# Re-laying the buffers behind the middle stage: eight output buffers for the last inverse products instead of four

## The chip, the cores and the metric

The kernel runs on one core of a Trainium2 chip. A core has a matrix engine (TensorE, PE in the profile; its weight loads stand apart as PEld), two elementwise engines (VectorE, DVE; ScalarE, ACT), GpSimd (POOL), and SyncE (SP), which here only issues DMAs. ACT and POOL issue DMAs too; ACTq and POOLq are their issues. Each engine works through its own instructions in the order of the program and stops at the first one whose inputs or buffers are not ready. Sixteen DMA engines move data between DRAM and the on-chip memory; matmul results land in PSUM banks, which an engine has to copy out.

The metric is the time of one execution in microseconds, lower being better; several runs are given as their median.

## What is computed

Two layers, A and B, each applied twice to `x` of 2048 rows and 576 columns, in the order A, B, A, B:

```python
x = x + _A_ref(_layernorm(x, axis=-1), ...)   # A: Cr @ (x Wr^T) - Ci @ (x Wi^T), a two-dimensional DFT's real part
x = x + _B_ref(_layernorm(x, axis=-1), B_k, B_v, B_shift_k, B_ssm_k, B_ssm_D)
# B: kv = (short convolution of k) * v
#    y  = (long causal convolution of kv with ssm_k, by FFT) + kv * ssm_D
#    return q * y                     # q is the layer-normed x
```

`y` depends on `k`, `v` and the convolution kernels alone, not on `x`. So it is worked out once, and used by both B layers.

## The kernel before

The long convolution (`branch()`) is woven into the first A layer (`layer()`). The A layer runs over 128 steps n: four blocks of 512 output rows, two parts (real and imaginary) and 16 row tiles. A step multiplies a row tile of `x`, kept in `mats` as a high and a low half, by one 128x512 piece of the DFT matrix: twelve matmuls of 512 columns into the PSUM tiles `s0` to `s3`, and two into `rm`. The DFT pieces are loaded by SP (`load_c`), one a step, and split into halves by ACT (line 98) and DVE (line 99). After each block come eight half pieces of `hidden()`, 27 matmuls of 288 columns each, with an addition by DVE on line 287.

The convolution goes through three stages: a first transform (up to step 42), the middle stage, and the last inverse. Middle and last stage are one list, `feeds`: 64 middle items (two column halves `hf`, 32 groups `qg`) and 32 last-inverse products (two halves, 16 columns `j`). Ten of the products stand between the later middle items. The other 22 follow the last middle item: six of half 0 and all sixteen of half 1. `branch()` is a generator, and the loop over the steps draws from it as the share of the A layer that has passed demands, so that it ends near step 111.

A middle item (`mid_kernel`, `mid_signal`, `mid_round`, `mid_inverse`, lines 520 to 549) uses two buffers `kk`, two `yf`, the constants `mc`, and an output buffer `vo` that it stores to `vd`.

A last-inverse product (`i2_products`, line 551) does, for each of its two 288-column pieces: two matmuls into a bank `bk`; a copy of that bank by ACT into a buffer `vo` (line 512 is the helper `act`, which keeps ACT's copies in their written order); a DMA from ACT's queue that writes one half of the buffer's partitions to `yb` in DRAM (line 561); and a DMA from POOL's queue that adds the other half onto the same rows of `yb` (line 564). The addition has to wait for the write, and the buffer is free again only when the addition has landed. A product therefore takes two `vo` buffers, of which there are four, one ring shared with the middle stage.

Its inputs: SP loads a column from `vd` into a `land` buffer (`load_feed`), ACT and DVE split it into `df` (lines 512 and 518), and POOL loads its coefficients into an `fc` buffer (`load_fc`, line 172).

After the products, `make_x1` gates the rows of `x` with `yb` (load on line 168, `gated` with lines 669 and 672), from step 113 on. The first two rows use buffers in `flts`, on the words that held `land`, `kk` and part of `vo`; later rows use the region `gate`, on the words of the middle stage's region `mid`. The tile `rt`, into which line 272 copies, and the third buffer of the DFT pieces (`craw`) lie on words of the four old `vo` buffers.

The program's order on each engine is not that of the source: a scheduler places the instructions by its own estimate of when each can run, and the hardware then keeps that order. `issue_after` and `behind` add orderings to it. Waits on DMAs go by a small set of semaphores that the DMAs of a kind take in turn.

The lines that the change touches stand in `branch()`, in the loop over `feeds`, under `if i == last_mid`:

Of the kernel before, what the change touches and what calls it, by code (L numbers as in the profile page):

```python
# [10 lines left out]
F32 = mybir.dt.float32  # L11
# [4 lines left out]
P = 128  # L16
HP = P // 2
S = 2048
D = 576
# [3 lines left out]
HD = D // 2  # L23
# [42 lines left out]
def fnet_h3_kernel(ctx: ExitStack, tc: tile.TileContext, x, c_mat, w_re, w_im, k_pad, v, shift_k,  # L66
# [45 lines left out]
    def flat(words, dt, name):  # L112
        return sb.tile([P, words], dt, tag=name, name=name)
# [4 lines left out]
    def region_b(dt, name):  # L118
        return sb.tile([P, 6 * WIDE], dt, tag="rb", name=name)
# [9 lines left out]
    ring = {}  # L129

    def lay(t, at, *sizes):

        for name, words, n in sizes:
            ring.setdefault(name, Ring()).tiles.extend(t[:, at + i * words:at + (i + 1) * words] for i in range(n))
            at += n * words
        assert at <= t.shape[1], (at, t.shape, sizes)
        return at

    def fresh(*names):
        for name in names:  # L140
            ring[name] = Ring()
# [14 lines left out]
    flts = flat(FLT, F32, "flts")  # L156
# [192 lines left out]
    def branch():  # L349
# [3 lines left out]
        at = lay(flts, SC_AT + CRAW * NT, ("so", D, 4), ("land", D, 3))  # L353
# [129 lines left out]
        m1 = region_b(FR, "mid")  # L483
        kk_at = SC_AT + CRAW * NT + 4 * D
        at = lay(m1, 0, ("df", 2 * D, 3), ("mc", 4 * P, 1))
        fresh("land", "fc")
        old = ring["craw"]
        held = [t for t in (old() for _ in range(3)) if t is not old.tiles[CRAW]]
        fresh("craw")
        ring["craw"].tiles.extend(held)  # L490
        spare = at
        at = lay(m1, at, ("yf", D, 2))
        fc_at = at
        at = lay(flts, SC_AT + CRAW * NT, ("res", D, 2))
# [25 lines left out]
        def mid_kernel(df):  # L520
            pk, kk = mid_half(df, HD), two(ring["kk"]())
            act(kk[:, 0, :], pk[:, :HD], AF.Copy)
            act(kk[lo, 1, :], kk[hi, 0, :], AF.Copy, scale=-1.0)
            act(kk[hi, 1, :], kk[hi, 0, :], AF.Copy)
            act(kk[hi, 0, :], kk[lo, 0, :], AF.Copy)
            return kk

        def mid_signal(df, kk):
            px = mid_half(df, 0)
            p1, p2 = kk[:, 0, :], kk[:, 1, :]  # L530
            nc.vector.tensor_tensor(p1, px[:, :HD], p1, OP.mult)
            nc.vector.tensor_tensor(p2[lo], px[hi, :HD], p2[lo], OP.mult)
            nc.vector.tensor_tensor(p2[hi], px[lo, :HD], p2[hi], OP.mult)
            nc.vector.tensor_tensor(p1, p1, p2, OP.add)
            return p1

        def mid_round(p1):
            yf = two(ring["yf"]())
            act_split(yf[:, 0, :], yf[:, 1, :], p1)
            return yf  # L540

        def mid_inverse(hf, qg, yf):
            pv = bank()
            mm(pv[:, :HD], mc[:, 2, :], yf[:, 0, :], True, False)
            mm(pv[:, :HD], mc[:, 2, :], yf[:, 1, :], False, False)
            mm(pv[:, :HD], mc[:, 3, :], yf[:, 0, :], False, True)
            vo = ring["vo"]()
            act(vo, pv[:, :HD], AF.Copy)
            nc.scalar.dma_start(v_d[hf][4 * qg:4 * qg + 4].rearrange("m j d -> (m j) d"), vo)

        def i2_products(hf, j, fc, vf):
            cols = slice(hf * HD, (hf + 1) * HD)
            late = []
            for i in range(2):
                ps, yo = bank(), ring["vo"]()
                cs = slice(i * HD, (i + 1) * HD)
                mm(ps[:, :HD], fc[:, i, :], vf[0][:, cs], True, False)
                mm(ps[:, :HD], fc[:, i, :], vf[1][:, cs], False, True)
                act(yo, ps[:, :HD], AF.Copy)
                to = yb_d[j][i::2, cols]  # L560
                nc.scalar.dma_start(to, yo[i * HP:(i + 1) * HP])
                late.append((to, yo[(1 - i) * HP:(2 - i) * HP]))
            for to, corr in late:
                nc.gpsimd.dma_start(to, corr, accum_op=OP.add)  # L564
# [13 lines left out]
        def load_feed(i):  # L578
            if i < len(feeds):
                kind, hf, q = feeds[i]  # L580
                landed[i] = ring["land"]()
                load_after(two(landed[i]) if kind else landed[i], v_d[hf][:, q::J, :] if kind else
                           t_d[4 * q:4 * q + 4, :, hf * D:(hf + 1) * D].rearrange("m j d -> (m j) d"))

        def load_fc(k):
            if k < len(rows):
                fcs[k] = two(ring["fc"]())
                load_fr(fcs[k], i2c[rows[k]])

        def split_feed(i):  # L590
            if i < len(feeds):
                halves[i] = parts("df")
                act_split(*halves[i], landed.pop(i))
# [10 lines left out]
        for i, (kind, hf, q) in enumerate(feeds):  # L604
            df = halves.pop(i)
            if kind:
                i2_products(hf, q, fcs.pop(used), df)
                load_fc(used + ahead)
                used += 1
            else:  # L610
                if len(yfs) == MID_LAG:
                    mid_inverse(*yfs.pop(0))
                    yield 0.4
                kk = mid_kernel(df)
                if product is not None:
                    yfs.append((*product[:2], mid_round(product[2])))
                yield 1.6
                product = hf, q, mid_signal(df, kk)
            split_feed(i + 2)
            if i >= I2_FIRST - 8 and feed_ahead == 3:  # L620
                tiles = [ring["land"]() for _ in range(3)]
                if tiles[0] is third:
                    ring["land"], feed_ahead = Ring(tiles[1:]), 2
                    lay(m1, fc_at, ("fc", 2 * P, 2))
                    load_fc(0)
                    load_fc(1)
            if feed_ahead == 2:
                feed_ahead = 2.5
            else:
                load_feed(i + int(feed_ahead) + 2)  # L630
            if i == last_mid:
                yield 0.4
                mid_inverse(*yfs.pop(0))
                yfs.append((*product[:2], mid_round(product[2])))
                while yfs:
                    yield 0.4
                    mid_inverse(*yfs.pop(0))
                for name, t, at, words in (("fc", m1, spare, 2 * P), ("land", flts, kk_at, D)):
                    old = ring[name]
                    held = [old.tiles[(old.n + m) % 2] for m in range(2)]  # L640
                    fresh(name)
                    lay(t, at, (name, words, 2))
                    ring[name].tiles.extend(held)
                for m in range(2):
                    load_fc(used + ahead + m)
                    load_feed(i + ahead + 3 + m)
                ahead = feed_ahead = 4
            yield I2_COST if kind else 1.1
# [101 lines left out]
    pending = []  # L750
    lay(flts, SC_AT, ("craw", NT, CRAW))
    br = branch()
    wl = load_w()
    load_x(0)
# [21 lines left out]
    for n, whole in layer(get_x0, lambda j: x[:, j, :], done0, pending):  # L776
# [3 lines left out]
        if (whole or whole is not None and n % J < J - 1) and n <= F1_END and not part:  # L780
            at = n if whole else n - 0.5
# [26 lines left out]
        if m == 0:  # L808
            lay(flts, SC_AT + CRAW * NT + 2 * D, ("xa", D, 2), ("yb", D, 2))
            old = ring["craw"]  # L810
            held = [old(), old()]
# [203 lines left out]
    for n, whole in layer(get_x1, lambda j: xb_d[j], done1, pending, 1):  # L1015
# [4 lines left out]
        if n == 0:  # L1020
            for name, at in (("xa", 0), ("yb", 4 * D)):
                old = ring[name]
# [5 lines left out]
        if n == STATIC:  # L1028
            t7.append(region_a(FR, "t7"))
            at = lay(flts, SC_AT + CRAW * NT, ("csum", WIDE, 3), ("rems", 2 * REM, 2))  # L1030
            lay(flts, SC_AT, ("csum", WIDE, 1))
            old = ring.pop("cs")
# [126 lines left out]
```

## Time and profile before

| What | Value |
|---|---|
| Median of 3 runs | 1223.32 us (1223.09 to 1223.67) |
| The profiled execution's own time | 1227.15 us |
| Its span | 1225.4 us |
| PE busy | 1179.6 us, 96% |
| DVE, ACT, POOL busy | 839.0, 671.8, 130.6 us |
| Mean DMA rate over the span | 212 GB/s |
| Granted TensorE clock, mean | 0.989 |

Times in the trace are microseconds from the span's start. "Idle before, releaser" says how long an engine stood still before an instruction and what ended the wait. In the chain of work that ended last, each step is followed back to what released it. Matmul ends are modelled, and a matmul's row (about 390 ns for 512 columns) is longer than the distance between two of them in a dense stream, so that short gaps can lie inside "busy". The granted clock is the share of full speed that TensorE was given.

### The profile page before, as it was taken

To read this page: it belongs to the slowest core of one execution; us is meant where nothing else is said; L and a number is where in the kernel's file an instruction comes from. 1 tells how busy PE (TensorE), PEld (TensorE's weight loads), DVE (VectorE), ACT (ScalarE), POOL (GpSimd) and SP (SyncE) were. 2 spreads that over 40 slices of the span, in tenths; PEclk is the share of its full clock that TensorE was granted. 3 is DMA by queue.
4 is the path that set the end of the run, shared out by engine and by line. 5 is a ranking of instruction groups with operands and counts; after the bars stand their busy time and mean duration, and the time that the engine had idled before them with its cause. 6 is when DMAs were issued, how large, how long until landed. Compare 5 with 4: busy or idle time off the path is not lost.

```text
span 1225.4 us, 18167 instructions
## 1 busy us (share of the span) xinstructions
PE 1179.6 (96%) x6184; PEld 992.8 (81%) x6184; DVE 839.0 (68%) x1498; ACT 671.8 (55%) x1343; POOL 130.6 (11%) x180
## 2 busy tenths in 40 slices
PE   7999999999999999997889999999999999999995
PEld 5776667988898888885668898888888888889995
DVE  7899973788877677762236756675776777775663
ACT  7855655688867778763344667544444445541200
POOL 2210000000000112104541111000000000001110
PEclk9999999999999999999889999999999999999998
DMA  9779898455666667558877777772682687895511
GB/s 338 279 218 312 265 291 257 148 161 176 216 205 204 188 182 211 176 182 214 192 169 227 244 242 245 251 265 91 178 290 90 198 279 259 260 319 173 195 68 39
DMA packets 152574, 260.37 MB, mean 212 GB/s; under 512 B 17185, under 2 KB 61473, under 8 KB 152482
## 3 DMA queue, kind: packets, MB, share of 16 engines
q1 hardware_dynamic: 106770, 205.45, 52.3%
q10 hardware_dynamic: 33680, 42.63, 10.2%
q0 software_dynamic: 12032, 11.15, 5.4%
q8 instruction: 48, 0.79, 0.2%
q14 instruction: 44, 0.36, 0.1%
HBM read 187.80 MB, written 71.37 MB: 211 GB/s over the span
## 4 chain that ended last, share of the span: by engine, by line
PE 47%; DMA 8%; DVE 3%; ACT 2%; issue 2%; POOL 0%; ACTq 0%; POOLq 0%; DVEq 0%; SPq 0%
PE s L75 28%; PE bk L75 18%; DMA yb<-flts 6%; PE rm L75 2%; ACT flts L512 1%; DVE mats L99 1%; DMA t<-ud 1%; ACT mats L98 0%; DMA flts<-td 0%; DMA flts<-vd 0%; DVE flts L181 0%; ACT u L98 0%; DMA y<-flts 0%; ACT mid L512 0%; DVE gate L669 0%
## 5 line engine op out<-in xcount | busy, mean ns | idle before, releaser
L75 PE MATMUL s<-mats 128*128 128x512 f32 x2088 | 546.8, 396 | 2.2 <-ACT mats L195 0.8
L75 PEld LDWEIGHTS s<-mats 128*128 128x128 f32 x2088 | 382.3, 189 | 85.0 <-issue 10.9
L99 DVE TENSOR_TENSOR mats<-flts,mats 128x512 fp32r<-128x512 f32 x206 | 140.8, 688 | 72.3 <-ACT mats L98 62.0
L98 ACT ACTIVATE mats<-flts 128x512 fp32r<-128x512 f32 x206 | 128.3, 628 | 79.8 <-PE bk L75 31.0
L75 PE MATMUL bk<-mid 128*128 128x288 f32 x704 | 132.5, 305 | 20.1 <-ACT flts L512 13.5
L75 PEld LDWEIGHTS bk<-mid 128*128 128x128 f32 x704 | 109.7, 189 | 47.3 <-ACT flts L512 23.5
L518 DVE TENSOR_TENSOR mid<-flts,mid 128x576 fp32r<-128x576 f32 (+1 forms) x149 | 93.6, 628 | 58.1 <-ACT mid L512 55.1
L512 ACT ACTIVATE flts<-bk 128x288 f32<-128x288 f32 x192 | 74.4, 405 | 104.5 <-DMA yb<-flts 47.3
L75 PE MATMUL bk<-w,u 128*128 128x288 f32 x864 | 124.2, 300 | 2.0 <-ACT w L240 1.0
L75 PEld LDWEIGHTS bk<-w,u 128*128 128x128 f32 x864 | 120.6, 192 | 6.6 <-ACT flts L512 2.9
L75 PE MATMUL rm<-mats 128*128 128x512 f32 x304 | 96.0, 393 | 0.0
L512 ACT ACTIVATE flts<-flts 64x288 f32<-64x288 f32 x192 | 85.0, 443 | 5.7 <-ACT flts L512 0.3
L512 ACT ACTIVATE mid<-flts 128x576 fp32r<-128x576 f32 (+1 forms) x148 | 80.1, 574 | 5.6 <-DMA flts<-td 2.1
L184 POOL TENSOR_TENSOR flts<-flts 128x1 f32<-128x1 f32 x35 | 29.3, 836 | 502.4 <-DVE flts L183 500.5
L451 ACT ACTIVATE flts<-bf 128x384 f32<-128x384 f32 (+1 forms) x104 | 43.2, 463 | 45.6 <-PE bf L75 45.5
L75 PE MATMUL bk<-mats 128*128 128x288 f32 (+1 forms) x376 | 67.8, 317 | 0.0
L75 PEld LDWEIGHTS rm<-mats 128*128 128x128 f32 x304 | 57.4, 189 | 11.9 <-issue 0.2
L75 PE MATMUL s<-t,mats 128*128 128x512 f32 x264 | 65.2, 390 | 0.1
L564 POOL DMA_DIRECT2D yb<-flts x64 | 54.0, 899 | 88.2 <-DMA yb<-flts 37.8
L75 PE MATMUL bk<-mats,t 128*128 128x288 f32 (+1 forms) x368 | 59.3, 303 | 0.0
L75 PEld LDWEIGHTS bk<-mats 128*128 128x128 f32 x376 | 55.6, 188 | 3.4
L75 PEld LDWEIGHTS s<-t,mats 128*128 128x128 f32 x264 | 49.4, 188 | 10.9 <-DVE t L99 0.7
(146 smaller groups left out, 1492.0 us busy)
## 6 DMA issues: line engine op xcount, KB each, us to landing
flts<-in_c_mat SPq DMA_DIRECT2D x148, 256.0 KB, 3.6
ph<-in_c_mat SPq DMA_DIRECT2D x54, 512.0 KB, 4.4
flts<-in_c_mat SPq DMA_DIRECT2D x30, 512.0 KB, 5.1
flts<-td SPq DMA_DIRECT2D x53, 288.0 KB, 3.0
td<-flts ACTq DMA_DIRECT2D x36, 384.0 KB, 4.6
vd<-flts ACTq DMA_DIRECT2D x64, 144.0 KB, 2.3
flts<-vd SPq DMA_DIRECT2D x32, 288.0 KB, 3.8
ud<-ph ACTq DMA_DIRECT2D x12, 512.0 KB, 6.4
```

The costliest lines, as they stand in the source:

```text
L75: return nc.tensor.matmul(ps, lhsT, rhs, start=first, stop=last, skip_group_check=more).ins
L98: a = nc.scalar.activation(h, src, AF.Copy).ins
L99: return a, nc.vector.tensor_tensor(l, src, h.bitcast(F32), OP.subtract).ins
L184: pows.append(nc.gpsimd.tensor_tensor(rs, ve, mhalf, OP.pow).ins)
L451: stored[:] = [nc.scalar.activation(so[:, i, :], ps[i], AF.Copy).ins]
L512: last_act.append(nc.scalar.activation(*args, **kw).ins)
L518: nc.vector.tensor_tensor(l, src, h.bitcast(F32), OP.subtract)
L564: nc.gpsimd.dma_start(to, corr, accum_op=OP.add)
```

## The change

When the last middle item is through, three kinds of its words are free: `yf` (1152 words a partition), `mc` (512) and `kk` (1152). Before, `yf` became two more `fc` buffers and `kk` two more `land` buffers. After the change, `mc` becomes the two `fc` buffers, `yf` the two `land` buffers, and `kk` four more `vo` buffers. The 22 products that follow have eight `vo` buffers, of which the new four are taken first. The number of `fc` and `land` buffers (four each) stays the same; no computing instruction and no DMA is added or removed.

```diff
                 while yfs:
                     yield 0.4
                     mid_inverse(*yfs.pop(0))
-                for name, t, at, words in (("fc", m1, spare, 2 * P), ("land", flts, kk_at, D)):
+                for name, t, at, words in (("fc", m1, spare - 4 * P, 2 * P), ("land", m1, spare, D)):
                     old = ring[name]
                     held = [old.tiles[(old.n + m) % 2] for m in range(2)]
                     fresh(name)
-                    lay(t, at, (name, words, 2))
+                    lay(t.bitcast(F32) if name == "land" else t, at, (name, words, 2))
                     ring[name].tiles.extend(held)
+                old = ring["vo"]
+                held = [old() for _ in range(4)]
+                fresh("vo")
+                lay(flts, kk_at, ("vo", HD, 4))
+                ring["vo"].tiles.extend(held)
                 for m in range(2):
                     load_fc(used + ahead + m)
                     load_feed(i + ahead + 3 + m)
```

## The prediction

> **What bounds the kernel now.** I read the page's busy times and its chain of waits first.
>
> ```profile
> PE 1179.6 (96%) x6184; PEld 992.8 (81%) x6184; DVE 839.0 (68%) x1498; ACT 671.8 (55%) x1343; POOL 130.6 (11%) x180
> PE s L75 28%; PE bk L75 18%; DMA yb<-flts 6%; PE rm L75 2%; ACT flts L512 1%; DVE mats L99 1%; DMA t<-ud 1%; ACT mats L98 0%; DMA flts<-td 0%; DMA flts<-vd 0%; DVE flts L181 0%; ACT u L98 0%; DMA y<-flts 0%; ACT mid L512 0%; DVE gate L669 0%
> ```
>
> TensorE is the bound over all, but the writes and additions into `yb` hold 6% of the chain, about 74 us of 1225.4, and they can only lie where the last inverse runs. So the next view is busy time by stretches: late middle stage, the 22 products from about 546 us, and what follows. The first number is the length, the others are each engine's busy time, and the last three are the granted clock, the DMA share and GB/s.
>
> ```profile
> 391.00:546.00 155.00, 153.26 (x840) 131.96 (x839) 112.45 (x216) 115.26 (x254) 23.02 (x31) 1.00 0.67 190
> 546.00:580.00 34.00, 26.54 (x143) 21.39 (x143) 8.46 (x13) 12.75 (x27) 14.75 (x21) 1.00 0.89 217
> 580.00:620.00 40.00, 32.05 (x149) 25.11 (x148) 10.42 (x16) 15.11 (x33) 21.03 (x28) 0.89 0.90 205
> 620.00:643.00 23.00, 19.87 (x96) 16.82 (x95) 7.67 (x12) 9.53 (x20) 9.87 (x13) 0.82 0.71 141
> 643.00:688.00 45.00, 44.84 (x198) 36.59 (x196) 28.14 (x73) 23.30 (x45) 7.92 (x13) 1.00 0.70 221
> ...
> 546.00:643.00 97.00, 78.47 (x385) 63.32 (x385) 26.56 (x39) 37.40 (x79) 45.65 (x61) 0.91 0.85 194
> ...
> 612.00:620.00 8.00, 4.91 (x18) 3.20 (x17) 1.28 (x2) 2.81 (x7) 3.07 (x4) 0.89 1.02 271
> ```
>
> PE is dense before 546 and after 643. Between them it is idle for 97.0 - 78.5 = 18.5 us even with modelled ends, no engine is full, and the clock drops. Who waits there:
>
> ```profile
> ACT flts L512 <- DMA yb<-flts: 47.3, 29, 3.1
> ...
> PE bk L75 <- ACT flts L512: 12.1, 13, 1.9
> ...
> PE bk L75 <- ACT mid L512: 6.3, 7, 1.9
> ```
>
> ACT stands for 47.3 us in front of a copy into `vo` until an addition has landed, PE for 18.4 us behind ACT. The chain in order of time (start, length) shows one turn of a buffer, then the last write; the timeline gives the first and last copy, the first matmul of step 112, and ACT's wait after the products:
>
> ```profile
> 550.02 2.57 DMA yb<-flts
> ...
> 557.31 4.42 DMA yb<-flts
> ...
> 562.28 3.42 DMA yb<-flts
> 565.73 0.04 issue
> 565.77 0.42 ACT flts L512
> 566.22 2.88 DMA yb<-flts
> ...
> 640.82 1.94 DMA yb<-flts
> ```
>
> ```profile
> 549.58 0.71 ACT L512 ACTIVATE flts<-bk 128x288 f32<-128x288 f32 x2 [2.88 <-DMA flts<-vd]
> ...
> 640.38 0.41 ACT L512 ACTIVATE flts<-bk 128x288 f32<-128x288 f32 x1
> ...
> 642.88 6.30 PE L75 MATMUL s<-mats 128*128 128x512 f32 x27
> ...
> 649.18 0.60 ACT L272 ACTIVATE flts<-rm 64x512 f32<-64x512 f32 x1 [8.39 <-DMA yb<-flts]
> ```
>
> A write is issued at 557.31, its addition at 562.28, the buffer is copied into again at 565.77 and the next write goes out at 566.22: a turn of 8.9 us. From the first copy to the last it is 640.38 - 549.58 = 90.8 us for 21 steps from product to product, 4.32 us each, or two products in 8.6 us. Four buffers, two a product, one turn: the ring is the bound.
>
> **The change, part by part.** Nothing is computed or moved more or less, so the price is in waits alone.
>
> *The added `vo` buffers.* With eight, a copy waits for the addition of four products back instead of two, and the built program's waits say so. A turn of 8.6 us would give 8.6 / 4 = 2.15 us a product. But the built order of ACT does not allow that. It puts the writes of a product behind the copies of the next one, sometimes the next two: the copies of product 5 and of product 7 stand before the last write of 5, and 7 needs the addition of 3. Followed through, a chain of such waits leads from product 3 to 15 in four turns, so three products a turn: 8.6 / 3 = 2.87 us. Three in flight also load the DMA engines and POOL's queue more than two, so I lengthen the turn by about 1.3 us to 9.9, which is an estimate inside what the chain of before shows (a single one of its DMA pieces runs from 2.57 to 4.42 us above). That gives 3.3 us a product.
>
> *What each engine would need.* Work by shapes in 546 to 643 (count | busy us, mean ns), and two dense runs of matmuls from a later stretch of the chain:
>
> ```profile
> L564 POOL DMA_DIRECT2D yb<-flts x43 | 36.6, 900 | 38.7 <-DMA yb<-flts 14.7 <-ACT flts L512 10.8 <-ACT mats L98 10.6
> L75 PE MATMUL s<-mats 128*128 128x512 f32 x117 | 35.4, 418 | 0.0
> L75 PE MATMUL bk<-w,u 128*128 128x288 f32 x158 | 25.1, 321 | 0.7 <-ACT flts L512 0.7
> ...
> L75 PE MATMUL bk<-mid 128*128 128x288 f32 x90 | 23.5, 343 | 17.9 <-ACT flts L512 11.5 <-ACT mid L512 6.3
> ...
> L512 ACT ACTIVATE flts<-bk 128x288 f32<-128x288 f32 x45 | 18.2, 410 | 52.6 <-DMA yb<-flts 47.3 <-DMA flts<-vd 2.9 <-PE bk L75 2.1
> ...
> L172 POOL DMA_DIRECT2D mid<-in_i2c x18 | 12.6, 714 | 14.5 <-PE bk L75 12.6 <-DMA yb<-flts 1.7 <-PE rm L75 0.2
> L75 PE MATMUL rm<-mats 128*128 128x512 f32 x20 | 7.7, 429 | 0.0
> ```
>
> ```profile
> 701.76 2.73 PE s L75 x12
> ...
> 704.95 3.60 PE bk L75 x27
> ```
>
> Dense, a matmul of 512 columns takes 2.73 / 12 = 0.228 us and one of 288 takes 3.60 / 27 = 0.133. So PE needs (117 + 20) x 0.228 + (158 + 90) x 0.133 = 31.2 + 33.0 = 64 us of the 97. POOL issues 36.6 + 12.6 = 49.2 us, or 2.2 a product. ACT is busy for 37.4 us; its 44 write issues take its turn as well, but stand partly beside its copies. None of these reaches 3.3 us a product.
>
> *From the pace to the time.* Call the pace p. In the built order the last product comes a step earlier than before: behind it PE still has two plus two matmuls of 512, a run of 27 and a full step of 14 before step 112 begins: 4 x 0.228 + 3.60 + 14 x 0.228 = 7.7 us, less about 0.5 for the copy that follows the product's matmuls. Step 112 then begins at 549.6 + 21p + 7.2, where it began at 642.9. The gain is 642.9 - 556.8 - 21p = 86.1 - 21p. With p = 3.3 it is 16.8 us. From 643 on PE is dense (44.8 of 45.0), so the gain is carried to the end.
>
> *`land` in place of `yf`, `fc` in place of `mc`.* The new `land` loads now wait, in SP's queue, for PE's last `mid_inverse`, as the new `fc` loads did before; behind them in SP's queue stand DFT pieces. Before, those loads waited for the last rounding, just ahead of that matmul. I take nothing: the half-1 loads next in the queue had to wait in any case for the last store to `vd`, which comes after the same matmul. Bounds: 0 to 2 us, one matmul wait of PE (1.9) at most. `mc` is free with the same matmul as `yf`: nothing.
>
> *The gating's first rows, `rt` and `craw`.* The first two rows load `yb` into the words of `kk`, which now hold the buffers of products 14 and 15, so these loads wait in SP's queue for the last additions, and DFT pieces from step 117 on stand behind. The addition that ACT waited for at 649.18 landed 8.8 us after the last copy at 640.38; 8.8 us after the new last copy is 1.6 us into step 112. Step 117 comes 5 x 14 x 0.228 = 16 us after 112 begins. So this wait is covered; if the cover were gone, each microsecond past it would cost one. `rt` and the third `craw` buffer lie on the old buffers, which are no longer the last ones used: ACT's wait of 8.4 us on line 272 shrinks to a microsecond or two. PE did not stand for it before, so I count nothing.
>
> Sum: -16.8 us in the profiled execution (1227.15, span 1225.4). The median stands 3.8 us below that execution: 1223.3 - 16.8 = 1206.5, say 1206.5.
>
> **Rivals.** *The other limits are lower than I think.* If later products find their buffers free and PE is all but dense, the 64 us of PE's work replace 97, a gain of 33 us at the very best. For it: none of the engines is full. Against it: three products a turn. With the turn unchanged, p = 2.87, the gain is 25.8 and the time 1197.5.
>
> *The DMA engines become the bound.* They are at 0.85 over the stage, 82 us of packets in 97. If packets keep their lengths and the share cannot pass 1.0, then with about 5 us of that traffic outside the products p is 77 / 22 = 3.5, or 3.73 if all of it counts; the gain is 12.6 or 7.8, the time 1210.7 or 1215.5. Against it: 8 us from 612 on moved 271 GB/s at 1.02, 1.4 times the stage's 194, so the lengths hold much waiting. [...]
>
> *Slower: packets lengthen under the crowding.* The same place; the price is 21 us for each microsecond of pace, and the break-even is p = 86.1 / 21 = 4.1, because the order leaves a whole step of PE's work behind the last product. It takes packets 4.1 / 3.73 = 1.10 times as long as now. With today's pace of 4.32 the time would be 1223.3 + 4.6 = 1227.9. Against it: 271 GB/s in the window above.
>
> *The change doesn't do what it says.* The waits of the built program have moved from two products back to four; only ACT's order could undo that, as priced.
>
> **How the numbers follow.** Pace from the turn, 3.1 to 3.5 us (1202 to 1211): 0.45. Close to the engines' limits, below 3.1 (1190 to 1202): 0.2. DMA-bound, 3.5 to 3.95 (1211 to 1220): 0.24. Above 3.95: 0.11, of which 0.04 within 0.2% (2.4 us, about what a measurement of this kernel can tell from no change) and 0.07 slower. So 0.89 faster, 0.04 the same, 0.07 slower. The range 1196 to 1218 leaves out about 0.06 below and 0.14 above.
>
> **What would show it.** ACT's wait for `yb` in the stage falls from 47 us to 15 or less; first to last copy takes about 69 us instead of 90.8; the DMA share of the stage rises above 0.95 and GB/s to about 240; the granted clock stays near 1.0; the wait on line 272 falls below 3 us; PE stays dense after step 112. I am wrong if ACT's wait for `yb` stays above 25 us (ACT's order or longer packets took the gain), if PE stands after step 112 for a DFT piece (SP held by the gating loads), or if POOL's additions queue behind `fc` loads that wait for PE.

## The result, and the profile after

| | Before | After |
|---|---|---|
| Median, same chip | 1223.49 us (1223.09 to 1225.22, 4 runs) | 1206.01 us (1205.11 to 1206.39, 4 runs) |
| Ratio, 95% interval | | 0.9853 (0.9836 to 0.987) |
| Profiled execution, its span | 1227.15, 1225.4 us | 1206.39, 1204.6 us |
| First to last copy of the 22 products | 90.8 us, 4.32 a product | 67.1 us, 3.19 a product |
| Step 112 begins | 642.88 us | 622.63 us |
| From there to the end of the span | 582.5 us | 582.0 us |

The change takes 17.5 us off the median, about 1.5%; 1206.5 was forecast. Two more pairs, each on a chip of its own, gave 1206.2 against 1225.49 (ratio 0.9843, 95% interval 0.9817 to 0.9869) and 1208.55 against 1226.41 (0.9851, 0.9829 to 0.9873).

The page of the kernel after: busy times, and the shares of the chain that ended last, by line.

```profile
PE 1169.3 (97%) x6184; PEld 989.5 (82%) x6184; DVE 838.6 (70%) x1498; ACT 669.8 (56%) x1343; POOL 129.7 (11%) x180
...
PE s L75 41%; PE bk L75 28%; PE rm L75 4%; DMA yb<-flts 3%; ACT flts L512 1%; ACT mid L512 1%; DMA t<-ud 1%; POOL yb L564 0%; DMA xa<-flts 0%; ACT u L98 0%; ACT mats L98 0%; ACTq L561 0%; DVE t L99 0%; POOLq L1160 0%; ACT t L98 0%
```

The writes and additions into `yb` hold 3% of the chain, where it was 6%. The same stretches as before: the stage now ends at 623 instead of 643.

```profile
391.00:546.00 155.00, 153.59 (x845) 132.62 (x844) 112.08 (x216) 115.40 (x254) 22.95 (x31) 1.00 0.67 191
546.00:580.00 34.00, 30.57 (x177) 26.17 (x177) 11.18 (x17) 16.57 (x37) 19.16 (x27) 1.00 1.03 263
580.00:623.00 43.00, 37.03 (x203) 32.19 (x202) 14.09 (x21) 18.44 (x42) 27.75 (x36) 0.96 0.99 225
546.00:623.00 77.00, 67.60 (x378) 58.36 (x378) 25.26 (x38) 35.02 (x78) 46.91 (x63) 0.98 1.01 242
623.00:668.00 45.00, 45.00 (x201) 37.26 (x200) 31.19 (x78) 24.20 (x46) 5.94 (x11) 1.00 0.69 226
```

In the stage PE is idle for 77.0 - 67.6 = 9.4 us instead of 18.5, and the DMA share is 1.01 instead of 0.85. The clock is 0.98 instead of 0.91, but this cannot be put down to the change: a second trace of the kernel before has 0.98 in its stage too (experiment 8). On both sides of the stage nothing has moved: 155 us with PE dense ahead of it, and 45.0 of 45.0 behind it. The waits in the stage after:

```profile
ACT flts L512 <- DMA yb<-flts: 18.6, 13, 4.5
POOL yb L564 <- DMA yb<-flts: 13.0, 10, 2.8
POOL mid L172 <- PE bk L75: 12.0, 6, 5.7
...
PE bk L75 <- ACT flts L512: 6.0, 4, 3.3
```

ACT's wait for a free buffer went from 47.3 to 18.6 us, and PE's wait for ACT's copies from 12.1 to 6.0. It did not go away: `yb` still holds 51% of the stage's chain (experiment 7), and 38% and 46% in two later traces of the kernel. The timeline after, from the first copy through the last one to step 112:

```profile
548.53 0.71 ACT L512 ACTIVATE flts<-bk 128x288 f32<-128x288 f32 x2 [2.88 <-DMA vd<-flts]
...
615.28 0.71 ACT L512 ACTIVATE flts<-bk 128x288 f32<-128x288 f32 x2 [1.98 <-PE bk L75]
...
618.50 0.33 SPq L168 DMA_DIRECT2D flts<-in_c_mat  x1
...
622.17 0.33 SPq L168 DMA_DIRECT2D flts<-yb  x1
...
622.63 2.88 PE L75 MATMUL s<-mats 128*128 128x512 f32 x12
...
623.00 0.60 ACT L272 ACTIVATE flts<-rm 64x512 f32<-64x512 f32 x1
...
627.38 1.08 SPq L168 DMA_DIRECT2D flts<-in_c_mat  x1
...
629.41 0.33 SPq L168 DMA_DIRECT2D flts<-yb  x1
```

A row with x2 is two copies in a row; the second of the pair at 615.28 starts at about 615.6, so the pace is (615.6 - 548.5) / 21 = 3.19 us. The copy on line 272 has no wait in front of it any more (8.39 us before).

### The profile page after: what moved, and what is told of

Read it like the earlier page. It is cut to its first block, busy times and chain, and to the rows that moved or that the text cites. A ratio compares the mean times of both kernels' runs of the same rounds, so it can differ in the third digit from the quotient of the medians.

```text
span 1204.6 us, 18174 instructions
## 1 busy us (share of the span) xinstructions
PE 1169.3 (97%) x6184; PEld 989.5 (82%) x6184; DVE 838.6 (70%) x1498; ACT 669.8 (56%) x1343; POOL 129.7 (11%) x180
## 4 chain that ended last, share of the span: by engine, by line
PE 73%; DMA 4%; ACT 2%; issue 1%; DVE 0%; POOL 0%; ACTq 0%; POOLq 0%; DVEq 0%
PE s L75 41%; PE bk L75 28%; PE rm L75 4%; DMA yb<-flts 3%; ACT flts L512 1%; ACT mid L512 1%; DMA t<-ud 1%; POOL yb L564 0%; DMA xa<-flts 0%; ACT u L98 0%; ACT mats L98 0%; ACTq L561 0%; DVE t L99 0%; POOLq L1160 0%; ACT t L98 0%
## 5 line engine op out<-in xcount | busy, mean ns | idle before, releaser
L75 PE MATMUL bk<-mid 128*128 128x288 f32 x704 | 129.8, 302 | 11.6 <-ACT flts L512 7.8
L75 PE MATMUL bk<-w,u 128*128 128x288 f32 x864 | 120.8, 295 | 0.4 <-DVE w L241 0.4
L75 PEld LDWEIGHTS bk<-w,u 128*128 128x128 f32 x864 | 117.3, 188 | 3.7 <-ACT flts L512 1.3
L518 DVE TENSOR_TENSOR mid<-flts,mid 128x576 fp32r<-128x576 f32 (+1 forms) x139 | 85.9, 618 | 26.5 <-ACT mid L512 20.1
L512 ACT ACTIVATE mid<-flts 128x576 fp32r<-128x576 f32 (+1 forms) x138 | 73.5, 568 | 4.4 <-DMA flts<-td 1.8
L75 PEld LDWEIGHTS rm<-mats 128*128 128x128 f32 x304 | 57.1, 188 | 12.1 <-issue 0.2
L287 DVE TENSOR_TENSOR flts<-flts,bk 128x288 f32<-128x288 f32 x48 | 21.7, 453 | 58.3 <-PE bk L75 58.2
```

Of the source, the lines that this page charges most:

```text
L75: return nc.tensor.matmul(ps, lhsT, rhs, start=first, stop=last, skip_group_check=more).ins
L287: added[:] = [nc.vector.tensor_tensor(r[:, cs], r[:, cs], ps[:, :HD], OP.add).ins]
L512: last_act.append(nc.scalar.activation(*args, **kw).ins)
L518: nc.vector.tensor_tensor(l, src, h.bitcast(F32), OP.subtract)
```

## Experiments

The kernels ran on several chips. On each of them the kernel before ran too, and each ratio, with its 95% interval in brackets, is to that.

**1. Undo the ring, keep the rest.** `land` on the words of `yf` and `fc` on those of `mc`, but `vo` stays at four: the change without these lines.

```diff
-                old = ring["vo"]
-                held = [old() for _ in range(4)]
-                fresh("vo")
-                lay(flts, kk_at, ("vo", HD, 4))
-                ring["vo"].tiles.extend(held)
```

> The changed kernel without its added output buffers: fc lies on mc, land on yf, the ring of output buffers stays at four. My reading of the result: the whole gain of 17 us is the ring's, and the re-lay of fc and land costs nothing, so 1222 to 1225 us, with a turn of 8.5 to 9 us for two products. Rival: the re-lay costs or saves something by itself (SP waiting for the last inverse matmul): then more than 3 us off the time of before, in either direction.

1225.57 us against 1226.6: 0.9988 (0.9976 to 1.0). Its pace is (638.66 - 550.27) / 21 = 4.21 us, beside 4.32 and 4.27 in two traces of before. So moving `land` and `fc` costs nothing that can be seen, and the gain is the ring's.

**2. Half of the ring.** Two new buffers instead of four.

```diff
-                lay(flts, kk_at, ("vo", HD, 4))
+                lay(flts, kk_at, ("vo", HD, 2))
```

> Six output buffers instead of eight (two new ones on kk's words). Turn theory (the pace is the turn of a buffer, copy to landed addition, over the products in flight, and ACT's written order takes about one of them away): two to two and a half products a turn of about 9.3 us, so 3.7 to 4.3 us a product, 1212 to 1221 us. DMA theory (the sixteen DMA engines are full at 3.2 to 3.5 us a product and set the pace): three products a turn of 8.6 us would be 2.9, already below the DMA limit, so as fast as with eight, 1205 to 1208 us.

1215.07 against 1226.6: 0.9907 (0.9887 to 0.9926), 0.9% where eight buffers gain 1.5%. The pace is (627.40 - 550.92) / 21 = 3.64 us, just under the 3.7 that I had put as the least. The stage with six buffers:

```profile
546.00:632.00 86.00, 71.38 (x391) 59.67 (x390) 26.13 (x40) 36.95 (x80) 47.79 (x63) 0.98 0.93 216
```

The DMA share is 0.93, below what eight buffers reach, and the pace is still set by the number of buffers. Had the DMA engines set it, six would have done nearly as well as eight.

**3. Let each write follow its copy on ACT.** My forecast said that ACT's order, with the writes of a product behind the copies of the next one or two, allows only three products a turn where four have buffers. This edit orders each write on ACT right behind its own copy, and the next copy behind the write:

```diff
-                nc.scalar.dma_start(to, yo[i * HP:(i + 1) * HP])
+                with tc.issue_after(last_act[-1]):
+                    last_act.append(nc.scalar.dma_start(to, yo[i * HP:(i + 1) * HP]).ins)
```

> Eight buffers, and each write into yb ordered on ACT right behind its copy, ahead of the next copies (in the changed kernel the writes of a product stand behind the copies of the next one or two). Turn theory: four products a turn instead of three; with the turn of about 10 us of the changed kernel 2.5 to 2.8 us a product, 7 to 10 us faster than the changed kernel, 1196 to 1200 us. DMA theory: the DMA share of the stage is at 1.0 already, nothing to gain, 1204 to 1208 us. Either could lose a little, since ACT now stands in line for each write's issue.

1198.66 against 1226.6: 0.9781 (0.976 to 0.9801), clearly below the 0.985 of the changed kernel. The time is inside what was expected, the pace is not: (615.54 - 551.43) / 21 = 3.05 us in the trace, where 2.5 to 2.8 was expected (the traced execution took 1202.86 us, 4.2 more than the median). What the built order does without this edit is seen in ACT's timeline of the kernel after:

```profile
578.19 0.41 ACT L512 ACTIVATE flts<-bk 128x288 f32<-128x288 f32 x1 [1.48 <-PE bk L75]
579.15 0.41 ACT L512 ACTIVATE flts<-bk 128x288 f32<-128x288 f32 x1 [0.56 <-DMA yb<-flts]
579.46 0.68 ACT L512 ACTIVATE mid<-mid 128x576 fp32r<-128x576 f32 x1
581.55 0.41 ACT L512 ACTIVATE flts<-bk 128x288 f32<-128x288 f32 x1 [1.41 <-DMA yb<-flts]
583.93 0.41 ACT L512 ACTIVATE flts<-bk 128x288 f32<-128x288 f32 x1 [1.97 <-DMA yb<-flts]
584.04 0.45 ACTq L561 DMA_DIRECT2D yb<-flts  x1
```

The product copied at 578.19 and 579.15 is ready at 579.6, but the first of its writes goes out at 584.04. Ahead of it in ACT's order stand both copies of the next product, and these wait for additions of earlier ones, 1.41 and 1.97 us. The finished buffers stand for 4.5 us before their transfers even begin. It is not one case: with the 44 copies and 44 writes of the stage's timeline paired in order, a write starts 3.1 us after its copy on average, 0.5 us in the kernel before and 0.5 us in the kernel with the edit. ACT's timeline of the kernel with the edit:

```profile
565.14 0.41 ACT L512 ACTIVATE flts<-bk 128x288 f32<-128x288 f32 x1 [1.25 <-PE bk L75]
565.58 0.45 ACTq L562 DMA_DIRECT2D yb<-flts  x1
566.16 0.41 ACT L512 ACTIVATE flts<-bk 128x288 f32<-128x288 f32 x1 [0.61 <-PE bk L75]
566.60 0.45 ACTq L562 DMA_DIRECT2D yb<-flts  x1
```

Each write goes out 0.44 us after its copy began. ACT's wait for a free buffer in the stage of this kernel:

```profile
ACT flts L512 <- DMA yb<-flts: 4.3, 5, 1.5
```

That is 4.3 us, where the kernel after has 18.6. It is the lowest of four traces with the writes ordered: the others, of experiments 5 and 6, have 5.0, 5.9 and 9.2.

**4. The same order with four buffers.** The edit of experiment 3 on the kernel before.

> The kernel before with four buffers and each write ordered right behind its copy. Turn theory: with four buffers a copy waits for the addition of two products back and the writes already stand behind their copies, so two products a turn as before: within 4 us of the kernel before, and most likely the same. Rival: the order alone, not the buffers, brings the gain of chained8 over the changed kernel: then 7 to 10 us faster than the kernel before.

1228.22 against 1225.49: 1.0026 (1.0011 to 1.0041), no gain and a small loss, at a pace of (637.27 - 548.08) / 21 = 4.25 us. ACT's timeline of the kernel before tells why there is nothing to mend:

```profile
556.87 0.41 ACT L512 ACTIVATE flts<-bk 128x288 f32<-128x288 f32 x1 [2.89 <-DMA yb<-flts]
557.31 0.45 ACTq L561 DMA_DIRECT2D yb<-flts  x1
558.77 0.41 ACT L512 ACTIVATE flts<-bk 128x288 f32<-128x288 f32 x1 [1.49 <-DMA yb<-flts]
559.21 0.45 ACTq L561 DMA_DIRECT2D yb<-flts  x1
```

With four buffers nearly every write follows its copy by 0.44 us already. The order that costs time came with the new buffers: in the built order of the changed kernel, copies that now have buffers stand ahead of the writes.

**5. Another order, for the reason of the gain.** Both copies of a product first, then both writes, and these ahead of the next product:

```diff
-            late = []
+            made, late = [], []
...
-                to = yb_d[j][i::2, cols]
-                nc.scalar.dma_start(to, yo[i * HP:(i + 1) * HP])
+                made.append((i, yo, yb_d[j][i::2, cols]))
+            for i, yo, to in made:
+                with tc.issue_after(last_act[-1]):
+                    last_act.append(nc.scalar.dma_start(to, yo[i * HP:(i + 1) * HP]).ins)
```

> Eight buffers; on ACT both copies of a product first, then both writes, then the next product (chained8 had copy, write, copy, write). Turn theory: what counts is that no write stands behind the next product's copies, so the same as chained8, about 0.978 of the kernel before; up to 2 us faster if ACT's standing in front of the first write of each pair (about 0.1 to 0.4 us a product) was on the path, up to 3 us slower if the later first write lengthens the turn.

1201.82 against 1225.49: 0.9806 (0.9777 to 0.9835); on the same chip the changed kernel took 1206.2. That is 4.4 us under the changed kernel, so it helps to keep the next product's copies behind the writes, whatever the order within a product. The interval takes in the 0.978 of experiment 3; whether the order within a product costs a few microseconds, these runs do not settle.

**6. Is it the products' order, or something earlier?** The edit of experiment 3 holds for the ten early products too, and its trace reaches the stage later: an early copy on line 272 starts at 261.15 us there, at 258.23 in the kernel after. So the edit on the 22 late products alone, beside the whole one again:

```diff
-                nc.scalar.dma_start(to, yo[i * HP:(i + 1) * HP])
+                with tc.issue_after(last_act[-1]):
+                    put = nc.scalar.dma_start(to, yo[i * HP:(i + 1) * HP]).ins
+                if hf or j >= J - I2_LATE:
+                    last_act.append(put)
```

> As chained8, but only for the 22 products behind the last middle item; the ten before it keep the scheduler's order. In chained8's trace the first copy of the 22 came at 552.4 us, in the changed kernel's at 548.5. If chaining the ten early writes costs that, this is 2 to 4 us faster than chained8; if those microseconds were lost before the stage for another reason (the traces differ already at 260 us), it is the same as chained8 within 2 us.

> Eight buffers with every write ordered right behind its copy, again. 0.977 to 0.981 of the kernel before, 5 to 9 us under the changed kernel, if the order of ACT's writes is what held the changed kernel at three products a turn. If its first comparison had luck with its chip, it comes out within 3 us of the changed kernel.

1199.24 for the late ones alone and 1198.7 for all, against 1226.41: 0.977 (0.9744 to 0.9797) and 0.978 (0.9757 to 0.9804). The changed kernel took 1208.55 on that chip, so the edit gains 9.3 to 9.9 us there. The late products alone give all of it. The 1 to 3 us by which some traces are late at 260 us come in kernels with and without the edit (260.28 with six buffers) and are not its work. The 552.4 us in the expectation is the start of the second copy in that trace; the first of the 22 products is copied at 551.43. The stage with the late products chained:

```profile
546.00:616.00 70.00, 67.96 (x390) 58.77 (x390) 26.24 (x40) 37.58 (x78) 46.20 (x61) 1.00 1.05 266
```

**7. Take DMA work away.** For the turn against the DMA engines: SP's sixteen loads of 288 KB that bring the half-1 columns of `vd` are left out, first in the changed kernel, then in that of experiment 3.

```diff
                 landed[i] = ring["land"]()
+                if kind and hf:
+                    return
```

> The changed kernel without SP's loads of the products of half 1 (16 loads of 288 KB left out; the products work on what lies in the buffers, so these rows of yb are not the reference's). That takes about 16 x 1.1 us of the 78 us of packets out of the stage. DMA theory: the pace follows the packets, 0.8 of 3.2 us, 2.5 to 2.6, until the matrix engine's 64 us bound it: 11 to 14 us faster than the changed kernel, 0.973 to 0.976 of the kernel before. Turn theory: the turn falls only as landings get shorter, from about 10 us to the 8.6 of the kernel before, 2.9 us a product: 5 to 8 us faster than the changed kernel, 0.979 to 0.981 of the kernel before. If landings stay as long as they are, no gain.

> chained8 without SP's loads of the products of half 1 (16 loads left out, so these rows of yb are not the reference's). In chained8 ACT stands only 4 us for a buffer, the DMA share is 1.03 and the pace 3.0 us a product. If the DMA engines bound it there, the stage falls by 5 us or more, towards the matrix engine's 64 us: 1190 to 1194 us, 0.972 to 0.975 of the kernel before. If the matrix engine and ACT bound it already, less than 3 us: 0.976 to 0.979.

In the changed kernel: 1200.66 against 1225.49, 0.98 (0.9774 to 0.9825), and 5.5 us under the changed kernel on that chip. The products hardly wait for the loads themselves: in the stage's chain of the kernel after no load of `vd` stands in two of its three traces, and one of 3.3 us in the third. Without the loads the landings are shorter. DMA issues in the stage, first the kernel after, then without the loads (KB each, median us from issue to landing):

```profile
yb<-flts ACTq DMA_DIRECT2D x44, 72.0 KB, 4.2
yb<-flts POOLq DMA_DIRECT2D x44, 72.0 KB, 4.4
```

```profile
yb<-flts ACTq DMA_DIRECT2D x44, 72.0 KB, 3.4
yb<-flts POOLq DMA_DIRECT2D x44, 72.0 KB, 3.9
```

A turn that is 0.8 + 0.5 = 1.3 us shorter, at three products a turn and 21 steps, is 21 x 1.3 / 3 = 9 us at the most; the pace fell from 3.19 to (610.74 - 549.24) / 21 = 2.93, which is 5.5 us. A gain of 11 to 14 us, which the rival of full DMA engines asked for, did not come; nor did as much packet time go as that rival counted on, 78 us less 0.94 x 71 = 67, or 11 us, where 16 x 1.1 = 18 was put.

With the order mended as well: 1193.62 against 1226.41, 0.9741 (0.9713 to 0.9769), 5.1 us under the whole chained kernel on that chip. I had put 5 us or more as the sign that the DMA engines bound that kernel. But the landings got shorter as well (4.8 + 5.2 us with the loads on that chip, 3.6 + 3.9 without them), and PE became full, so this run does not tell the engines' load from the length of the turn. Its stage and the chain of its stage by line:

```profile
546.00:610.00 64.00, 63.89 (x370) 55.80 (x369) 26.35 (x39) 37.41 (x78) 46.56 (x61) 1.00 0.97 211
```

```profile
by line: PE bk L75 49.9%; PE s L75 43.0%; PE rm L75 7.2%; issue 0.2%
```

PE is busy for 63.89 of 64 us, and step 112 begins at 609.31: this is the 64 us of PE's work that the forecast took from before's trace as the least for the stage. For comparison the stage's chain of the kernels before and after, of experiment 3's kernel, and of its second run in experiment 6:

```profile
by line: DMA yb<-flts 69.4%; PE bk L75 8.5%; issue 6.8%; ACT flts L512 4.1%; DMA flts<-vd 3.9%; PE s L75 2.2%; POOL yb L564 1.6%; POOL mid L172 1.2%; ACT mats L98 0.8%; ACT u L98 0.6%; ACTq L561 0.5%; POOLq L564 0.5%; ACTq L512 0.2%; ACT mi
```

```profile
by line: DMA yb<-flts 50.6%; PE bk L75 14.1%; PE s L75 13.9%; issue 6.5%; ACT flts L512 4.4%; POOL yb L564 3.5%; PE rm L75 2.8%; ACTq L561 1.9%; ACT mid L512 0.8%; POOL mid L172 0.6%; ACT mats L98 0.4%; POOLq L564 0.2%; ACTq L512 0.2%; POOL
```

```profile
by line: PE bk L75 38.7%; PE s L75 20.2%; DMA flts<-in_c_mat 10.1%; DMA mid<-in_i2c 8.8%; DMA yb<-flts 7.5%; PE rm L75 2.8%; ACT flts L512 2.8%; issue 2.8%; ACTq L562 1.9%; POOL yb L565 1.6%; ACT mid L512 1.0%; DVE mats L99 1.0%; ACT mats L
```

```profile
by line: DMA yb<-flts 41.9%; PE bk L75 12.2%; DMA flts<-in_c_mat 8.6%; PE s L75 6.1%; issue 5.5%; ACT flts L512 5.3%; DMA flts<-vd 4.9%; ACTq L562 3.9%; POOL yb L565 3.1%; ACT mid L512 3.0%; POOL mid L172 2.0%; PE rm L75 1.3%; DVE mid L518 
```

So the writes and additions fall from 69.4% of the stage's chain before to 50.6% after. What bounds the stage once the order is mended is not settled: the two traces of the same chained kernel give `yb` 7.5% and 41.9%, with landings of DFT pieces and other loads beside it in both, at nearly the same pace (3.05 and 2.99). Without the loads it is PE.

**8. The same two kernels again.** Once more before, and the changed kernel twice on other chips.

> The kernel before, profiled a second time. Its first profiled execution took 1227.15 us, 3.8 over the median, and showed a granted clock of 0.91 in the stage of the products. If that slowness lies in the stage (longer turns, lower clock), a profiled execution nearer 1223 us shows the first matmul of step 112 some 3 us earlier than 642.9; if it lies elsewhere, step 112 begins at 642.9 again.

> The changed kernel once more, on the chip of this call, so that the order experiments stand beside it: 0.985 of the kernel before, as in its first comparison. Without it the gain of chaining the writes (0.9781 against 0.9853) would rest on two different sets of runs.

> The changed kernel again, beside the next two on one chip: 0.984 to 0.986 of the kernel before.

The kernel before took 1226.16 beside a median of 1226.6, no nearer to 1223 than the first traced execution, so the run does not decide what it was meant to. Its trace reaches step 112 at 641.12, 1.8 us earlier than the first one did, and it is 1.0 us shorter in its span (1224.4). One trace is no more exact than that, so a difference under 2 us between two traces shows nothing here. What the trace does show is the clock of the stage:

```profile
546.00:641.00 95.00, 73.30 (x383) 58.06 (x382) 26.71 (x39) 37.37 (x79) 45.43 (x60) 0.98 0.87 198
```

It is 0.98 where the first trace had 0.91, at a pace of 4.27 beside 4.32. So the pace of the ring hardly follows that clock. The changed kernel's times stand in the section above.

**All of it in one table.** The landings and the pace are read from the traces. A buffer's turn is an estimate: 8.6 us, which is two of before's paces at its 3.3 + 3.8 = 7.1 us of landings, plus what the two landings are longer or shorter in that stage. The last column is that turn divided by the measured pace: how many products go through in a turn. Before's 2.0 is therefore put in, not found.

| Kernel | write + addition, us | turn, us | pace, us | products a turn |
|---|---|---|---|---|
| before, four buffers | 3.3 + 3.8 | 8.6 | 4.32 | 2.0 |
| four, re-laid (1) | 3.2 + 3.7 | 8.4 | 4.21 | 2.0 |
| four, chained (4) | 3.4 + 3.9 | 8.8 | 4.25 | 2.1 |
| six (2) | 3.6 + 4.3 | 9.4 | 3.64 | 2.6 |
| eight, after | 4.2 + 4.4 | 10.1 | 3.19 | 3.2 |
| eight, without loads (7) | 3.4 + 3.9 | 8.8 | 2.93 | 3.0 |
| eight, chained (3) | 4.6 + 4.9 | 11.0 | 3.05 | 3.6 |
| eight, chained again (6) | 4.8 + 5.2 | 11.5 | 2.99 | 3.8 |
| eight, chained in pairs (5) | 4.7 + 5.0 | 11.2 | 2.94 | 3.8 |
| eight, chained late (6) | 4.7 + 5.2 | 11.4 | 2.91 | 3.9 |
| eight, chained, without loads (7) | 3.6 + 3.9 | 9.0 | 2.76 | 3.3, PE full |

Eight buffers are four products. ACT's order holds them to about three a turn, and six buffers, which are three products, to 2.6; with the order mended eight give 3.6 to 3.9, but the turn has grown by another microsecond, with more transfers in flight; without the loads, PE is full before four a turn can be reached.

The turn of the table leaves out the time that a finished copy stands behind other copies. With it the count closes: in the kernel after a write starts 3.1 us behind its copy, 2.6 more than before, so a buffer is held for about 10.1 + 2.6 = 12.7 us, and 12.7 / 3.19 = 4.0 products. With six buffers it is 2.1 us, 1.6 more, and (9.4 + 1.6) / 3.64 = 3.0 products. In both the buffers are all in use, and ACT's order costs the fourth product by holding them longer.

The chained kernels of experiments 3 and 6, which leave nothing out, are faster than both kernels of this comparison: 0.977 to 0.978 of before.

## Why the prediction was right

**The bound.** That four buffers and one turn of write and addition set the pace is shown: with nothing else changed in the ring, four, six and eight buffers give 4.21, 3.64 and 3.19 us a product, and re-laying the rest gives nothing.

**Three a turn, 3.3 us.** Measured 3.19, 3.2 products a turn by the estimate of the table. The two estimates in the forecast hold: landings 1.5 us longer where the turn was put 1.3 longer, which makes a turn of 10.1 where 9.9 was put. That ACT's order keeps it from four is shown by experiments 3, 5 and 6: mended, it gave 4 to 10 us on the chips where the changed kernel ran beside it, and 3.6 to 3.9 products a turn.

**From the pace to the time.** The formula gave step 112 at first copy + 21 p + 7.2. The last term measured 622.63 - 615.6 = 7.0. The gain in the stage was 642.88 - 622.63 = 20.25 us, where 16.8 was forecast: 21 x (3.30 - 3.19) = 2.3 us is the pace, which was put too long, 1.05 us is the first copy, which came earlier (549.58 to 548.53), and 0.1 is the rest. Two traces of one kernel differ by nearly 2 us at this place (experiment 8), so the split is rough.

**The sum against the median.** The median fell by 17.5 us and lies 0.5 from the forecast. That it is so close is luck; the steps were not as exact. The profiled execution of before lay 3.7 us above its median, that of after 0.4. I subtracted a gain worked out in one execution from the median, and so the gain that I had put 3.4 us too small met an execution that was 3.7 us too long. With the stage of before's second trace (641.12) the gain is 18.5 us.

**`land`, `fc` and the gating's loads.** Nothing was counted, and nothing shows. POOL's `fc` loads wait for PE 12.0 us in the stage, 12.6 before, so the additions that stand behind them in POOL's order lose no more than they did. The gating's loads of `yb` are issued at 622.17 and 629.41, with DFT pieces behind them, and PE is busy for 45.0 of the 45 us from 623 on. From step 112 to the end of the span it is 582.0 us, 582.5 before.

**Signs that were named.** DMA share above 0.95: 1.01. About 240 GB/s: 242. Clock near 1.0: 0.98, which says nothing, since a trace of before has it too. First to last copy 69 us: 67.1. Line 272 below 3 us: no wait. One was missed: ACT's wait for `yb`, 15 us or less, was 18.6, and 21.4 and 26.4 in the two later traces of the kernel; in the last of these it passes the 25 us that I had named as a sign of being wrong, at the same pace ((615.4 - 547.8) / 21 = 3.22). The paces of the three traces lie within 0.03 us, so the sum of ACT's waits, which differs by 8 us between them, was a poor sign to name; why it differs so stays open.

**The rivals.** The case of DMA engines at their limit put the pace at 3.5 to 3.73 us. Two of its terms were off. The packets' time fell from 0.85 x 97 = 82 us to 1.01 x 77 = 78, for 18.8 and 18.6 MB. And 10 of those 78 us lie outside the stretch from first to last copy, most of them behind the last one, where the rival put 5 us or none:

```profile
546.00:548.50 2.50, 2.50 (x21) 2.50 (x21) 0.23 (x1) 0.00 (x0) 0.06 (x1) 1.00 0.98 300
548.50:615.60 67.10, 57.70 (x315) 49.12 (x315) 21.85 (x33) 31.70 (x72) 42.22 (x57) 0.97 1.01 242
615.60:623.00 7.40, 7.40 (x45) 6.75 (x44) 3.18 (x5) 3.31 (x8) 4.62 (x6) 1.00 1.02 216
```

With these numbers a share that cannot pass 1.0 would give (78 - 10) / 21 = 3.24 us, next to the measured 3.19. So the changed kernel's time alone does not tell the turn from full DMA engines. The experiments do: six buffers stand at a share of 0.93 and are slower, and the late products chained stand at 1.05 over 70 us and 266 GB/s and are faster. The Trainium skill ("DMA: Bandwidth & Descriptors", section "Issuing engines are not separate DMA queues") says that DMAs run on the same sixteen engines, whichever engine starts them, and interleave. The runs agree: ACT's 72 KB writes land in 3.3, 4.2 and 4.6 us as more is in flight, and in 3.4 again when SP's loads are left out. Here it is a price on the turn and not a wall. The slower case, a pace over 4.1 from longer packets, did not come near: landings grew by 21%, but with 3.2 instead of 2.0 products in flight. The fast case, PE all but dense and 33 us, was reached only with the order mended and the loads left out, in the last kernel of experiment 7: step 112 at 609.31, which is 33.6 us earlier than before.

## What to carry to other kernels

When a ring of buffers sets the pace, price more buffers as the turn divided by the products that the issuing engine's order lets through, not by the number of buffers. Look in the timeline whether a transfer that frees a buffer stands behind work that waits for a buffer: a scheduler that is given more buffers may put such work ahead of the transfer, as in this kernel, so the order has to be read again after the ring has grown. Lengthen the turn by what the extra transfers in flight add to each landing, and ask which engine's plain work is the floor underneath.

## What the hardware showed that I had not expected

The mean share of the sixteen DMA engines can stand above 1.0 over a whole stage: 1.05 over 70 us at 266 GB/s, as the window of the kernel with the late products chained shows. So a share near 1.0 in the profile is no proof that the engines are full; what told the load here was the landing time of one kind of transfer.

The granted clock fell to 0.82 at the end of before's stage, although the single waits of PE there were short (18.4 us in 20 waits of 1.9 us at the most, by the two rows that the forecast quotes). It does not follow the idle time either: the second trace of the same kernel has PE idle for 95.0 - 73.3 = 21.7 us of its stage, more than the 18.5 of the first, and a clock of 0.98 instead of 0.91. What sets it there stays open.
